# Splitting weights and values side by side: high and low parts interleaved, and another place for columns and values in each step

## The chip, the cores and the metric

The kernel runs on one core of a Trainium2 chip. The core has five engines with instruction streams of their own: TensorE (PE; its weight loads are listed apart as PEld), VectorE (DVE), ScalarE (ACT), GpSimd (POOL) and SyncE (SP), which issues transfers. They share the on-chip memory SBUF (128 partitions) and, for matmul results, PSUM. The metric is device microseconds of one execution.

## The reference, cut to what matters

An attention with random features (8 batches, 8 heads, 576 tokens, 64 values a head) is followed by a mixture of 8 experts, of which each token takes one. The change lies in the experts:

```python
x = attn_out.transpose(0, 2, 1, 3).reshape(B * S, H * D)      # 4608 x 512
logits = x @ w_gate
expert_idx = argmax(logits, axis=1)
gate_w = softmax(logits)[token, expert_idx]
for e in range(8):
    xe = x[expert_idx == e]
    h = maximum(xe @ w1[e], 0)        # 512 -> 1024
    out[expert_idx == e] = gate_w * (h @ w2[e])   # 1024 -> 512
```

All of it is fp32, and the result must be fp32 in precision.

## The kernel before, in words

The attention takes the first 270 us or so. Its tokens are written to a table in DRAM and sorted into slots by expert. The expert part then goes in steps. A step takes two blocks of 128 tokens of one expert, in a few cases three, and consists of:

- the gather of the blocks (POOL, line 855), their transposes on TensorE (line 871), and the columns: `columns` splits the transposed tokens into a high part `xh` (ScalarE, line 52) and a low part `xl` = value - high (VectorE, line 46);
- layer one, `l1`: for each of 8 slices of 128 hidden units, `products` (line 894) issues 12 matmuls into a PSUM bank: for each of 4 pieces of the 512 inputs, high weights by high columns and low weights by high columns, and then high weights by low columns. The weights are the operand that is loaded into the array, the columns (256, or 384 in a step of three blocks) are the moving operand. Lines 912 and 913 make the values: the high part `hh` by Relu on ScalarE, and the low part `hl` on VectorE, which subtracts the high part from the clipped sum;
- layer two, `l2`, for each block: 24 matmuls of 512 columns (lines 920 to 922). Here the values are what is loaded, and w2 moves: `hh` by `w2h`, `hh` by `w2l`, `hl` by `w2h`, for each of 8 pieces;
- the scaling by the gate (lines 933 and 934) and the scatter to the output (line 935).

High and low parts are of type fp32r, a form of fp32 that TensorE takes in one pass; three products of parts stand for one fp32 product. The first step's layers (lines 810 and 819) use plain fp32 instead.

The weights of an expert come by DMA into `w1s` and `w2s` (2 MB each) and are split by `split` into `w1p0`, `w1p1` (high and low of w1) and `w2p0`, `w2p1`, in 8 casts and 8 subtractions each. The order of instructions on each engine is the order of the code: in a step, `l1` of this step, then `begin` of the next (its transposes, its columns, and the split of w1 when its expert is another), then `l2` of this step. Semaphore waits are put in from the addresses that the instructions touch. The layers are written out for each step, so that addresses can differ from step to step; before, they do not. The tiles are laid one behind the other in SBUF, with two unused ones, `pad0` and `pad1`, that shift what follows.

Of the kernel before, what the change touches and what calls it, by code (L numbers as in the profile page):

```python
# [8 lines left out]
F32 = mybir.dt.float32  # L9
F32R = mybir.dt.float32r  # L10
# [8 lines left out]
P = 128  # L19
B, H, S, D, M = 8, 8, 576, 64, 128  # L20
DM = H * D
E, F = 8, 1024
# [22 lines left out]
def sub_r(nc, eng, lo, src, hi):  # L45
    eng.tensor_tensor(out=lo, in0=src, in1=hi.bitcast(F32), op=ALU.subtract)


def split_r(nc, hi, lo, src, eng_hi, eng_lo):

    if eng_hi is nc.scalar:
        nc.scalar.copy(hi, src)  # L52
    else:
        eng_hi.tensor_copy(hi, src)
    sub_r(nc, eng_lo, lo, src, hi)


class Attention:
# [318 lines left out]
    def run(self, pre):  # L377
        units = [(b, h) for b in range(B) for h in [-1] + list(range(H))]
        n, rt = len(units), self.routing
        tr = lambda i: self.unit_tr(*units[i]) if i < n else pre.rows(i - n) if i < n + 2 else None  # L380
        th = lambda i: self.unit_th(*units[i]) if i < n else None
        self.start(units)
        for b in range(B):
            i = b * (2 * NP + 1)
            if b:
                self.rest(units, i, b, pre, tr, th)
            if b + 1 < B:
                self.load_rest(b + 1)
                self.load_main(b + 1)
            for k in range(0 if b else 2, NP):  # L390
                self.pair(units, i + 1 + 2 * k, b * NP + k, pre, tr, th)
                if k == (0 if b else 2) and b + 1 < B:
                    self.load_v(b + 1)
        p = B * NP - 1
        self.pair_kv(p)
        rt.some(3)
        self.pair_fold(p - 1)
        self.unit_t(*units[n - 2])
        self.pair_fold(p, "kv")
        self.pair_nu(p - 1, 0)  # L400
        self.pair_x(p - 1, 0)
        self.unit_t(*units[n - 1])
        self.pair_nu(p - 1, 1, "tr")
        self.pair_x(p - 1, 1)
        self.pair_nu(p, 0)
        self.pair_nu(p, 1)
        self.cq.close()
        pre.banks()
        for a in range(2):
            self.pair_x(p, a)  # L410


class Routing:
# [71 lines left out]
    def bank(self, name):  # L485
        return self.ps.tile([P, 512], F32, name=name, tag=self.tag)
# [271 lines left out]
class Experts:  # L758
# [3 lines left out]
    NC, NF, T2, T3 = DM // P, F // P, 2 * P, 3 * P  # L762
# [108 lines left out]
            self.nc.tensor.transpose(p[:, c * P:(c + 1) * P], x[:, c * P:(c + 1) * P], self.ident)  # L871
        self.nc.gpsimd.tensor_copy(gate, x[:, DM:DM + 1])  # L872

    def columns(self, a, p):
        s = slice(a * P, (a + 1) * P)
        split_r(self.nc, self.xh[:, :, s], self.xl[:, :, s], p.rearrange("p (c t) -> p c t", t=P),
                self.nc.scalar, self.nc.vector)

    def xtrans(self, t):
        for a in range(2):  # L880
            self.turn(2 * t + a, self.p_x[a])
            self.columns(a, self.p_x[a])

    def third(self):
        self.turn_rows(self.x3, self.p_1[3], self.gt[6])
        self.columns(2, self.p_1[3])

    def products(self, f, o, k):

        NC, c = self.NC, slice(f * P, (f + 1) * P)  # L890
        h, l = self.xh[:, :, k], self.xl[:, :, k]
        ops = [(w, h, i) for i in range(NC) for w in (self.w1h, self.w1l)] + [(self.w1h, l, i) for i in range(NC)]
        for k, (w, x, i) in enumerate(ops):
            self.nc.tensor.matmul(o, w[:, i, c], x[:, i, :], start=k == 0, stop=k == len(ops) - 1)  # L894

    def l1(self, t, n):

        for g in range(4 if n == self.T2 else self.NF):
            if t == 1 and g < 4:
                self.split(2, range(2 * g, 2 * g + 2))  # L900
            p = self.p_1[g % 4]
            if n == self.T2:
                fs = slice(2 * g, 2 * g + 2)
                o = p.rearrange("p (f t) -> p f t", t=n)
            else:
                fs = slice(g, g + 1)
                o = p[:, :n].unsqueeze(1)
            for k, f in enumerate(range(fs.start, fs.stop)):
                for c in (slice(0, self.T2), slice(self.T2, n)) if n > self.T2 and g == 0 else (slice(0, n),):
                    self.products(f, o[:, k, c], c)  # L910
            a, b = self.hh[:, fs, :n], self.hl[:, fs, :n]
            self.nc.scalar.activation(a, o, AF.Relu)  # L912
            self.nc.vector.scalar_tensor_tensor(out=b, in0=o, scalar=0.0, in1=a.bitcast(F32), op0=ALU.max,  # L913
                                                op1=ALU.subtract)

    def l2(self, t, a):
        nc, k = self.nc, slice(a * P, (a + 1) * P)
        h, l, p = self.hh, self.hl, self.p_2[a % 2]
        for c in range(self.NF):
            nc.tensor.matmul(p, h[:, c, k], self.w2h[:, c, :], start=c == 0, stop=False)  # L920
            nc.tensor.matmul(p, h[:, c, k], self.w2l[:, c, :], start=False, stop=False)  # L921
            nc.tensor.matmul(p, l[:, c, k], self.w2h[:, c, :], start=False, stop=c == self.NF - 1)  # L922
        if a == 2:
            self.send(p, self.y3, self.gt[6], self.idx[:, 2 * NPR + t:2 * NPR + t + 1])
        else:
            self.store(2 * t + a, p, self.idx)
# [31 lines left out]
    def step(self, t, following):  # L958
        engines = (ET.PE, ET.DVE, ET.Activation, ET.Pool)
        two = self.reg(5, t, 1, engines)  # L960
        with self.tc.If(two > 0) as pair:  # L961
            self.l1(t, self.T2)
        with pair.Else():
            self.third()
            self.l1(t, self.T3)
        if t + 2 < NPR:
            self.gather(t + 2)
        if t + 1 < NPR:
            self.gather3(t + 1)
        if t == 1:  # L970
            self.next(0, 2)
        following()
        self.nc.gpsimd.drain()  # L973
        with self.tc.If(two > 0) as pair:  # L974
            self.l2(t, 0)
            self.when(self.reg(4, t, 1, engines), lambda: self.l2(t, 1))
        with pair.Else():
            for a in range(3):
                self.l2(t, a)
# [11 lines left out]
    def run(self, ctx):  # L991
        nc, rt = self.nc, self.rt
        cp = ctx.enter_context(self.tc.tile_pool(name="mo_c", bufs=1))
        NC, NF, T2 = self.NC, self.NF, self.T2
        bank = lambda n, tags: [self.ps.tile([P, 512], F32, name=f"{n}{i}", tag=g) for i, g in enumerate(tags)]
        self.p_2 = bank("p_2", ("tr", "nu"))
        self.p_x = bank("p_x", ("kv", "t2"))
        ring = lambda n, sh, dt, k: [cp.tile(sh, dt, name=f"{n}{i}") for i in range(k)]
        cp.tile([P, 88], F32, name="pad0")
        (self.w1h, self.w1l), (self.w2h, self.w2l) = (ring(n, [P, c, w], F32R, 2) for n, c, w in  # L1000
                                                      (("w1p", NC, F), ("w2p", NF, DM)))
        self.h0 = cp.tile([P, NF, T2], F32, name="h0")
        self.hh, self.hl = (cp.tile([P, NF, self.T3], F32R, name=n) for n in ("hh", "hl"))
        cp.tile([P, 48], F32, name="pad1")
        self.xh, self.xl = (cp.tile([P, NC, self.T3], F32R, name=n) for n in ("xh", "xl"))
        self.ys = ring("ys", [P, DM], F32, 3)
        xg = ring("xgm", [P, ROW], F32, 2)
        self.x3, self.y3 = cp.tile([P, ROW], F32, name="x3"), cp.tile([P, DM], F32, name="y3")
        for x in xg + [self.x3]:
            nc.gpsimd.memset(x, 0.0)  # L1010
        self.xg = self.xg + xg

        rt.slots(cp, (self.p_2[0], self.p_x[0], self.p_x[1]), self.idx, lambda: self.fill(22))
        self.fill(32)
        self.gather(1)
        self.gather3(1)
        self.gather(2)
        for g in range(4):
            self.relu0(g)
        rt.plan(self.flags)  # L1020
        self.split(1)
        self.next(0, 1)
        self.l20(0)
        self.xtrans(1)
        self.l20(1)
        for t in range(1, NPM - 1):
            if t > 1:
                self.change(t, 2)
            self.step(t, lambda: self.begin(t + 1))
        self.tail(NPM - 1)  # L1030
# [45 lines left out]
```

## Time and profile before

| | us |
|---|---|
| three runs: lowest, median, highest | 729.4, 730.23, 730.68 |
| the profiled execution | 732.33 |
| its span, first to last instruction | 730.6 |
| TensorE busy | 706.3 (97%) |
| VectorE busy | 380.4 (52%) |
| ScalarE busy | 325.5 (45%) |
| GpSimd busy | 256.4 (35%) |

The duration of a matmul in the profile is the time from its start to its modelled end, and matmuls overlap; what a matmul takes of the time is the distance from its start to the start of the next. In a row of the timeline that merges several instructions, the second number is the time from the start of the first to the end of the last.

### The profile page before, as it was taken

Reading aid. Unit: us, or ns where it says so; the run is one execution under the profiler, and the core shown is the slowest. Engines: PE = TensorE matmul, PEld = TensorE weight load, DVE = VectorE, ACT = ScalarE, POOL = GpSimd, SP = SyncE. Lnnn points to the kernel's source line nnn. Section 1 sums busy time; section 2 is a strip of 40 time slices with the busy share of each in tenths; the row PEclk is TensorE's granted clock in tenths of the full one; section 3 lists DMA queues with packets and bytes.
Section 4 is the critical chain, followed back from the end, with each engine's and each line's share of the span. In section 5 each row is a group of like instructions: output and inputs, shape, how many; then the busy total and the mean of one; then the engine's idle time right before and its main releaser. Section 6 shows DMA issues by size and latency. Waiting matters only on the chain. (4 is left out here: it accounts for less than half of the span.)

```text
span 730.6 us, 18640 instructions
## 1 busy us (share of the span) xinstructions
PE 706.3 (97%) x6985; PEld 632.5 (87%) x6985; DVE 380.4 (52%) x860; ACT 325.5 (45%) x950; POOL 256.4 (35%) x459
## 2 busy tenths in 40 slices
PE   7999999999999999999999999999998999999995
PEld 6898889888888887788999889998987989989994
DVE  4689899899899888722221245212343245122220
ACT  6877887877778735411221144212342144111210
POOL 7555555555546633221222112221112303211221
PEclk9999999999999999999999999999999999999998
DMA  8944735626633611551111026121144125201000
GB/s 209 261 121 114 215 109 157 196 69 197 196 115 121 227 62 40 182 174 37 46 52 59 32 83 230 61 70 37 31 144 168 61 85 194 80 31 34 17 32 22
DMA packets 69502, 79.82 MB, mean 109 GB/s; under 512 B 28398, under 2 KB 52974, under 8 KB 69360
## 3 DMA queue, kind: packets, MB, share of 16 engines
q1 hardware_dynamic: 61136, 58.81, 26.1%
q0 software_dynamic: 7680, 19.04, 7.9%
q8 instruction: 82, 1.34, 0.8%
q14 instruction: 60, 0.49, 0.2%
q10 hardware_dynamic: 544, 0.13, 0.1%
HBM read 64.79 MB, written 19.55 MB: 115 GB/s over the span
## 5 line engine op out<-in xcount | busy, mean ns | idle before, releaser
L894 PE MATMUL p<-xh,w1p 128*128 128x256 f32 (+2 forms) x1104 | 159.5, 287 | 0.9 <-ACT xh L52 0.9
L894 PEld LDWEIGHTS p<-xh,w1p 128*128 128x128 f32 x1104 | 146.0, 189 | 2.9 <-ACT xh L52 1.3
L935 POOL DMA_INDIRECT out_dram<-ys,idx x36 | 36.9, 1026 | 305.4 <-DVE ys L934 213.3
L913 DVE SCALAR_TENSOR_TENSOR hl<-p,hh 128x512 fp32r<-128x512 f32 (+1 forms) x76 | 50.1, 662 | 135.2 <-ACT hh L912 133.0
L920 PE MATMUL p<-w2p,hh 128*128 128x512 f32 x288 | 114.3, 397 | 3.1 <-DVEq L940 2.7
L921 PE MATMUL p<-w2p,hh 128*128 128x512 f32 x288 | 112.9, 392 | 0.0
L922 PE MATMUL p<-w2p,hl 128*128 128x512 f32 x288 | 112.8, 392 | 0.0
L912 ACT ACTIVATE hh<-p 128x512 fp32r<-128x512 f32 (+1 forms) x76 | 43.8, 576 | 142.6 <-PE p L894 140.1
L934 DVE TENSOR_SCALAR ys<-p,gt 128x256 f32<-128x256 f32 x36 | 17.4, 482 | 153.1 <-ACT ys L933 153.1
L186 ACT ACTIVATE kp<-pp,mx 128x128 f32<-128x128 f32 x256 | 76.2, 417 | 44.5 <-DVE mx L176 29.2
L933 ACT ACTIVATE ys<-p,gt 128x256 f32<-128x256 f32 x36 | 17.1, 476 | 170.9 <-PE p L922 103.2
L894 PE MATMUL p<-xl,w1p 128*128 128x256 f32 (+2 forms) x552 | 90.7, 287 | 0.0
L176 DVE TENSOR_REDUCE mx<-pp 128x8 f32<-128x1024 f32 x64 | 76.9, 1214 | 7.7 <-PE pp L169 4.5
L186 ACT ACTIVATE qp<-pp,mx 128x128 f32<-128x128 f32 x256 | 78.4, 457 | 0.0
L203 POOL TENSOR_TENSOR k<-kp 128x256 f32<-128x256 f32 x64 | 46.7, 730 | 88.2 <-ACT kp L186 81.7
L894 PEld LDWEIGHTS p<-xl,w1p 128*128 128x128 f32 x552 | 77.4, 190 | 0.1
L169 PE MATMUL pp<-om_t,th 64*128 64x128 f32 x1024 | 70.8, 283 | 1.3 <-ACT th L156 0.7
L169 PEld LDWEIGHTS pp<-om_t,th 64*128 64x128 f32 x1024 | 61.6, 187 | 9.8 <-issue 5.5
L920 PEld LDWEIGHTS p<-w2p,hh 128*128 128x128 f32 x288 | 54.4, 189 | 14.3 <-issue 3.5
L922 PEld LDWEIGHTS p<-w2p,hl 128*128 128x128 f32 x288 | 54.5, 189 | 11.6
L921 PEld LDWEIGHTS p<-w2p,hh 128*128 128x128 f32 x288 | 54.5, 189 | 10.9
L264 PE MATMUL nu<-kva,qt 128*64 128x73 f32 x1024 | 42.9, 229 | 3.7 <-ACT kva L251 3.5
(370 smaller groups left out, 1086.9 us busy)
## 6 DMA issues: line engine op xcount, KB each, us to landing
w1s<-in_moe_w_dram SPq DMA_DIRECT2D x5, 2048.0 KB, 8.7
w2s<-in_moe_w_dram SPq DMA_DIRECT2D x5, 2048.0 KB, 10.3
v<-in_v_dram SPq DMA_DIRECT2D x32, 256.0 KB, 5.5
token_rows<-xc SPq DMA_DIRECT2D x8, 1024.0 KB, 5.1
k<-in_k_dram SPq DMA_DIRECT2D x31, 256.0 KB, 5.1
q<-in_q_dram SPq DMA_DIRECT2D x31, 256.0 KB, 5.5
kr<-in_k_dram SPq DMA_DIRECT2D x16, 64.0 KB, 2.6
vz<-in_v_dram SPq DMA_DIRECT2D x16, 64.0 KB, 5.6
```

Source lines behind the costliest of these rows:

```text
L169: nc.tensor.matmul(pp[:, a, n, i, :], th[r, c], self.om[r, :], start=True, stop=True)
L176: nc.vector.tensor_reduce(out=mx[:, :, n], in_=s[("pp", h)][:, :, n], axis=AX.X, op=ALU.max, negate=True)
L186: nc.scalar.activation(x[:, j, :], pp[:, j % 2, n, j // 2, :], AF.Exp, bias=mx[:, j % 2, n, j // 2:j // 2 + 1])
L203: add = lambda o, x, y: nc.gpsimd.tensor_tensor(out=o, in0=x, in1=y, op=ALU.add)
L264: nc.tensor.matmul(o[r, j, :], qt[:, j, r], kva[:, a, :], start=True, stop=True)
L894: self.nc.tensor.matmul(o, w[:, i, c], x[:, i, :], start=k == 0, stop=k == len(ops) - 1)
L912: self.nc.scalar.activation(a, o, AF.Relu)
L913: self.nc.vector.scalar_tensor_tensor(out=b, in0=o, scalar=0.0, in1=a.bitcast(F32), op0=ALU.max, op1=ALU.subtract)
L920: nc.tensor.matmul(p, h[:, c, k], self.w2h[:, c, :], start=c == 0, stop=False)
L921: nc.tensor.matmul(p, h[:, c, k], self.w2l[:, c, :], start=False, stop=False)
L922: nc.tensor.matmul(p, l[:, c, k], self.w2h[:, c, :], start=False, stop=c == self.NF - 1)
L935: self.nc.gpsimd.indirect_dma_start(out=self.out[:, :], in_=y, in_offset=None, bounds_check=NT - 1, out_offset=bass.IndirectOffsetOnAxis(a ...
```

## The change: high and low side by side, and a place that moves

w1's two parts become one tile, in which the low part of each element stands right behind its high part. The values' two parts are joined in the same way. Both are read and written through views with a step of two elements; the values between them are the other part. w2's parts and the columns' parts stay tiles of their own. The columns `xh`, `xl` and the values `hp` get 128 elements more, and in step t they begin at an offset within these: a multiple of 8 elements (32 bytes) given by (t - 1) * 3 mod 16 for the columns and (t - 1) * 5 mod 16 for the values. The order of the tiles in SBUF changes (columns ahead of the values).

```diff
+    def col(self, t):
+        o = (t - 1) * 3 % 16 * 8
+        return [x[:, o:o + self.NC * self.T3].rearrange("p (c n) -> p c n", n=self.T3) for x in (self.xh, self.xl)]
+
+    def mid(self, t):
+        o = (t - 1) * 5 % 16 * 8
+        x = self.hp[:, o:o + self.NF * self.T3 * 2].rearrange("p (f n s) -> p f n s", n=self.T3, s=2)
+        return x[:, :, :, 0], x[:, :, :, 1]
+
-    def columns(self, a, p):
+    def columns(self, t, a, p):
         s = slice(a * P, (a + 1) * P)
-        split_r(self.nc, self.xh[:, :, s], self.xl[:, :, s], p.rearrange("p (c t) -> p c t", t=P),
+        split_r(self.nc, *(x[:, :, s] for x in self.col(t)), p.rearrange("p (c t) -> p c t", t=P),
                 self.nc.scalar, self.nc.vector)
...
-    def products(self, f, o, k):
+    def products(self, t, f, o, k):
 
         NC, c = self.NC, slice(f * P, (f + 1) * P)
-        h, l = self.xh[:, :, k], self.xl[:, :, k]
+        h, l = (x[:, :, k] for x in self.col(t))
...
-            a, b = self.hh[:, fs, :n], self.hl[:, fs, :n]
+            a, b = (x[:, fs, :n] for x in self.mid(t))
             self.nc.scalar.activation(a, o, AF.Relu)
...
     def l2(self, t, a):
         nc, k = self.nc, slice(a * P, (a + 1) * P)
-        h, l, p = self.hh, self.hl, self.p_2[a % 2]
+        (h, l), p = self.mid(t), self.p_2[a % 2]
...
         cp.tile([P, 88], F32, name="pad0")
-        (self.w1h, self.w1l), (self.w2h, self.w2l) = (ring(n, [P, c, w], F32R, 2) for n, c, w in
-                                                      (("w1p", NC, F), ("w2p", NF, DM)))
+        w1p = cp.tile([P, NC, F, 2], F32R, name="w1p")
+        self.w1h, self.w1l = w1p[:, :, :, 0], w1p[:, :, :, 1]
+        self.w2h, self.w2l = ring("w2p", [P, NF, DM], F32R, 2)
+        cp.tile([P, 48], F32, name="pad1")
+        self.xh, self.xl = (cp.tile([P, NC * self.T3 + P], F32R, name=n) for n in ("xh", "xl"))
         self.h0 = cp.tile([P, NF, T2], F32, name="h0")
-        self.hh, self.hl = (cp.tile([P, NF, self.T3], F32R, name=n) for n in ("hh", "hl"))
-        cp.tile([P, 48], F32, name="pad1")
-        self.xh, self.xl = (cp.tile([P, NC, self.T3], F32R, name=n) for n in ("xh", "xl"))
+        self.hp = cp.tile([P, NF * self.T3 * 2 + P], F32R, name="hp")
```

The instructions of each engine stay the same and in the same order. Only waits on ScalarE and VectorE differ, since they follow from addresses. On ScalarE, where a step begins the next one (the two casts of columns, then the casts of w1), the program before has:

```order
L52 CAST xh<-p_x_5515 128x4x128 [waits DVE_49,PE_49]
L52 CAST xh<-p_x_5516 128x4x128 [waits DVE_49,PE_49]
L843 TENSOR_LOAD flags
L940 COMPARE_AND_BRANCH
L52 CAST w1p_5518<-w1s 128x512 [waits DMAHW3_49,DMAHW5_49,DMAHW1_49,DMAHW7_49,DVE_49,Activation_49]
L52 CAST w1p_5518<-w1s 128x512 [waits DVE_49,Activation_49] x7
```

The same place now, in one of the steps:

```order
L52 CAST xh<-p_x_5515 128x4x128 [waits DVE_49,PE_49,Activation_49]
L52 CAST xh<-p_x_5516 128x4x128 [waits PE_49]
L843 TENSOR_LOAD flags
L949 COMPARE_AND_BRANCH
L52 CAST w1p<-w1s 128x512 [waits DMAHW5_49,DMAHW7_49,DMAHW3_49,DMAHW1_49]
L52 CAST w1p<-w1s 128x512 x7
```

A cast of columns now waits for ScalarE's own earlier work (in most steps the second of the two, here the first), and the casts of w1 no longer name VectorE and ScalarE.

## Rows read from the trace of the kernel before

**Rows 1.** The page: busy time by engine, and TensorE's granted clock in 40 slices.
```profile
PE 706.3 (97%) x6985; PEld 632.5 (87%) x6985; DVE 380.4 (52%) x860; ACT 325.5 (45%) x950; POOL 256.4 (35%) x459
PEclk9999999999999999999999999999999999999998
```

**Rows 2.** Busy time by stretch: stretch, length, engines, granted clock, DMA share, GB/s.
```profile
300.00:350.00 50.00, 50.00 (x339) 46.20 (x338) 15.27 (x26) 13.73 (x26) 12.69 (x16) 1.00 0.38 131
...
461.11:472.43 11.32, 11.32 (x97) 11.28 (x96) 2.56 (x4) 2.27 (x4) 4.36 (x6) 1.00 0.23 72
438.10:449.45 11.35, 11.35 (x98) 11.31 (x96) 7.28 (x12) 6.43 (x12) 4.81 (x6) 1.00 0.61 219
```

**Rows 3.** Groups, shapes kept apart: count, busy us, mean ns, idle before.
```profile
L894 PE MATMUL p<-xh,w1p 128*128 128x256 f32 x976 | 135.4, 282 | 0.0
...
L920 PE MATMUL p<-w2p,hh 128*128 128x512 f32 x288 | 114.3, 397 | 3.1 <-DVEq L940 2.7 <-PEq L940 0.4
...
L894 PE MATMUL p<-xl,w1p 128*128 128x256 f32 x488 | 77.4, 281 | 0.0
...
L894 PE MATMUL p<-xh,w1p 128*128 128x384 f32 x112 | 21.9, 337 | 0.0
...
L894 PE MATMUL p<-xl,w1p 128*128 128x384 f32 x56 | 12.0, 336 | 0.0
```

**Rows 4.** Timeline, layer one of 256 columns: start us, us, engine, group.
```profile
462.75 1.10 PE L894 MATMUL p<-xh,w1p 128*128 128x256 f32 x8
...
466.52 0.64 PE L894 MATMUL p<-xl,w1p 128*128 128x256 f32 x4
...
469.82 1.10 PE L894 MATMUL p<-xh,w1p 128*128 128x256 f32 x8
```

**Rows 5.** Timeline, layer two: the third matmul of two triples.
```profile
452.95 0.39 PE L922 MATMUL p<-w2p,hl 128*128 128x512 f32 x1
...
461.11 0.39 PE L922 MATMUL p<-w2p,hl 128*128 128x512 f32 x1
```

**Rows 6.** Timeline, steps of three blocks: first groups, then groups of 384 columns.
```profile
508.92 0.62 PE L894 MATMUL p<-xl,w1p 128*128 128x256 f32 x4
...
572.34 0.62 PE L894 MATMUL p<-xl,w1p 128*128 128x256 f32 x4
...
577.09 1.55 PE L894 MATMUL p<-xh,w1p 128*128 128x384 f32 x8
...
587.49 1.55 PE L894 MATMUL p<-xh,w1p 128*128 128x384 f32 x8
```

**Rows 7.** Timeline, weight loads: plain fp32 of 512 columns, one each; transposes.
```profile
293.60 0.19 PEld L819 LDWEIGHTS p<-w2s,h 128*128 128x128 f32 x1 [0.24 <-issue]
...
298.75 0.19 PEld L819 LDWEIGHTS p<-w2s,h 128*128 128x128 f32 x1 [0.24 <-issue]
...
472.55 0.89 PEld L871 LDWEIGHTS p_x<-ident,xgm 128*128 128x128 f32 x8
```

**Rows 8.** VectorE reductions, by line: duration min/median/max; L490's elements lie 288 bytes apart.
```profile
L490 DVE TENSOR_REDUCE rt_L<-x x8: 620/623/628, 52.3 to 269.1; 128x32 f32<-128x256 f32 x8
L696 DVE TENSOR_REDUCE f_tt<-rt_L x1: 453/453/453, 276.1 to 276.1; 128x36 f32<-128x288 f32 x1
```

**Rows 9.** Timeline, what covers ScalarE and VectorE around the two layers.
```profile
292.11 4.89 DVE L46 TENSOR_TENSOR w1p<-w1s,w1p 128x512 fp32r<-128x512 f32 x8
...
297.32 1.27 DVE L46 TENSOR_TENSOR xl<-p_x,xh 128x512 fp32r<-128x512 f32 x2
...
299.21 1.51 PE L894 MATMUL p<-xh,w1p 128*128 128x256 f32 x8
...
450.43 0.69 DVE L913 SCALAR_TENSOR_TENSOR hl<-p,hh 128x512 fp32r<-128x512 f32 x1 [2.14 <-ACT hh L912]
...
592.03 4.89 DVE L46 TENSOR_TENSOR w1p<-w1s,w1p 128x512 fp32r<-128x512 f32 x8
...
606.79 0.99 PE L894 MATMUL p<-xh,w1p 128*128 128x256 f32 x7
```

More of the change, by code (lines that the diff above doesn't have):

```diff
@@ L881, in xtrans, with third @@
             self.turn(2 * t + a, self.p_x[a])
-            self.columns(a, self.p_x[a])
-    def third(self):
+            self.columns(t, a, self.p_x[a])
+    def third(self, t):
         self.turn_rows(self.x3, self.p_1[3], self.gt[6])
-        self.columns(2, self.p_1[3])
-    def products(self, f, o, k):
+        self.columns(t, 2, self.p_1[3])
+    def products(self, t, f, o, k):
         NC, c = self.NC, slice(f * P, (f + 1) * P)
-        h, l = self.xh[:, :, k], self.xl[:, :, k]
+        h, l = (x[:, :, k] for x in self.col(t))
         ops = [(w, h, i) for i in range(NC) for w in (self.w1h, self.w1l)] + [(self.w1h, l, i) for i in range(NC)]
@@ L909, in l1 @@
                 for c in (slice(0, self.T2), slice(self.T2, n)) if n > self.T2 and g == 0 else (slice(0, n),):
-                    self.products(f, o[:, k, c], c)
-            a, b = self.hh[:, fs, :n], self.hl[:, fs, :n]
+                    self.products(t, f, o[:, k, c], c)
+            a, b = (x[:, fs, :n] for x in self.mid(t))
             self.nc.scalar.activation(a, o, AF.Relu)
@@ L963, in step @@
         with pair.Else():
-            self.third()
+            self.third(t)
             self.l1(t, self.T3)
```

## The prediction

> **What bounds the kernel now.** I read the page's busy shares first, then the busy time by stretches, then the groups with shapes kept apart, and last single stretches of the timeline, because only those give the distance from one matmul to the next. TensorE is busy for 97% of the span and its clock is at the higher level (2.4 GHz) in nearly every slice [rows 1]. In the expert part, from about 299 us to the end, it is busy 50.00 of 50 us, while VectorE has 15.27 and ScalarE 13.73 [rows 2]. So the only thing that can move the end by much is how closely the matmuls of the two expert layers follow each other. The reader is to take three distances from the rows:
>
> - First layer, 256 columns: a group of 12 matmuls starts at 462.75 and the sixth group at 469.82, so 7.07 us / 60 = 117.8 ns [rows 4]. There are 976 + 488 = 1464 of them [rows 3].
> - First layer, 384 columns (the steps of three blocks): (587.49 - 577.09) / 60 = 173.3 ns [rows 6]; 112 + 56 = 168 matmuls [rows 3].
> - Second layer, 512 columns: twelve triples from 452.95 to 461.11, so 8.16 us / 36 = 226.7 ns [rows 5]; three lines of 288, so 864 matmuls [rows 3].
>
> From 384 to 512 columns the distance grows by 53.4 ns for 128 columns, 0.417 ns a column, which is one column a cycle of 2.4 GHz. Then 512 columns need 213.3 ns, and 13.4 ns a matmul are something else. The plain fp32 matmuls of line 819 (512 columns as well, with a weight load of the same size before each) follow each other every (298.75 - 293.60) / 12 = 429.2 ns [rows 7], and twice 213.3 is 426.7: only 2.5 ns over. So the 13.4 ns are no fixed price of changing weights; they come up where the moving operand is read at a column a cycle while the next weights are being read. A weight load alone needs (0.89 - 0.14) / 7 = 107 ns for 128 elements, by the transposes [rows 7]. At 256 columns load and matmul are about equally long (107 and 106.7), both disturb each other, and the distance is 117.8.
>
> Two more rows tell what this disturbance is like. It does not depend on the other engines: the step at 438.10 has 7.28 us of VectorE, 6.43 of ScalarE and DMA at 0.61, the one at 461.11 has 2.56, 2.27 and 0.23, and both take 11.3 us for their 96 matmuls [rows 2]. And it is not one number: at the start of the two three-block steps, with the same addresses, four matmuls take 0.62 us where a usual group takes 0.64 [rows 4, 6]; less the 0.28 us of the last one, that is 113 ns a matmul against some 120 (rounding leaves 3 ns either way). So the distance depends on how the two reads happen to stand to each other in time.
>
> **The change, part by part.** No instruction is added, removed or moved on any engine; PE, POOL and SP keep their waits too. What changes is where three tiles lie, and the step between elements.
>
> (a) The weight operand of both expert layers (w1 in the first, the values in the second) is read with a step of two elements. Per matmul the weight read then passes over 1024 bytes in place of 512. At 107 ns that is 9.6 bytes per ns, just what the moving read does (2048 bytes in 213.3 ns). No row shows a weight read with such a step, so its price needs bounds. From below: two reads of equal pace that collide once are out of each other's way from then on, where reads at a ratio of 1 to 2 meet again and again. If the excess goes to the 2.5 ns of line 819, the second layer wins 10.9 x 864 = 9.4 us and the 384-column matmuls 10.9 x 168 = 1.8 us. At 256 columns the nearest row is the 113 ns, which wins 117.8 - 113.3 = 4.5 x 1464 = 6.6 us; the lowest end is the transposes' 107, 10.8 x 1464 = 15.8 us. Sum: -17.8 us, at most -27. From above: VectorE's reduction of line 490 reads single elements 288 bytes apart in 623 ns for 256, and line 696 reads 288 adjoining ones in 453 [rows 8]: 2.43 against 1.57 ns an element, a factor of 1.55. With it a weight load takes 166 ns. That lies below the second layer's 226.7, but the first layer waits for it: 59 x 1464 = +86 us, and nearly nothing at 384 columns. I take the gain, since the rows of TensorE lie nearer than a VectorE row with 36 times the step.
>
> The Trainium skill ("SBUF — State Buffer", the section on Door 1, the note on cachelines) says that SBUF is read in lines of 16 bytes and that two hits a line suffice for full speed. A step of two fp32 leaves just two, so by it the +86 us do not arise; no run here shows it. A second rule speaks against my gain: by "TensorE: Matmul & The Clock Gate", Part 2, weights have a read port of their own and loading them takes no read bandwidth from the running matmul. By it there is nothing to win and the time stays at 730; the 13.4 ns beside the 2.5 ns disagree with it as far as they go.
>
> (b) ScalarE and VectorE write w1 and the values, and VectorE reads the high part back, with the step of two. With the factor of 1.55 a w1 subtraction goes from 0.60 us (4.89 / 8) to 0.95, eight of them 2.7 us longer. In the loop that ends at 599.6 in place of 596.9, and the next first layer starts at 606.79 [rows 9]: hidden under the second layer. At the first step the eight start at 292.11, the low columns follow until 298.59, and the first matmul starts at 299.21 [rows 9]; the low columns are wanted after eight matmuls (1.51 us less the last one's tail), so about 0.8 us would show. The low part of the last pair of values ends at 450.43 + 0.69 = 451.1 [rows 9], and its first matmul is the 19th of 48, at 461.11 - 29 x 0.2267 = 454.5: 0.6 us more is covered by the 18 before it. I take 0 for (b), with +0.8 as the other end.
>
> (c) Columns and values start at another multiple of 32 bytes in each step. Nothing is computed for it at run time. Tiles of neighbouring steps now overlap at shifted places, so one cast of columns waits for the cast before it on its own engine, which could cost the overlap of the two, some 0.1 us a step, behind which the subtraction and then the w1 casts stand; all of it lies beside the second layer's 11 us. Its other effect is on how the two reads stand to each other. The two levels at equal addresses, 113 and 118, bound it: between -6.6 us, which (a) already has, and nothing.
>
> (d) The waits that w1 and w2 casts lose were on work long done; 0.
>
> Sum: 732.3 (the profiled execution) - 17.8 = 714.5. The median of the three runs is 2.1 us below the profiled one, so I say **712.5 us**. Within this case 703 (the transposes' level) to 723 (only half of it comes).
>
> **The rivals.**
>
> Nothing changes. If the 13.4 ns come from the type of the operands alone, an element read costs the same wherever it lies, and (b) is hidden: 730.2 us. For it: the distance of 117.8 is the same in steps with quite different traffic [rows 2]. Against it: 113 ns at the same operands [rows 6]. The first rule against the gain leads here.
>
> Slower: each piece of memory that the weight read opens costs the moving read something, and with the step of two it opens twice as many. Place: every expert matmul. Price: the excess doubles, 13.4 x (864 + 168) = 13.8 us, and in the first layer 117.8 - 107 = 10.8 x 1464 = 15.8 us; 732.3 + 29.6 - 2.1 = 760 us. It decides from the point where the reads do not fall into step; if it holds for a part of the steps only, the time lies between 732 and 760. For it: the excess exists only where both reads run. Against it: other engines' reads cost TensorE nothing, so that not simply any further access does.
>
> Slower by much: the read with the step takes 1.55 times as long (+86 us, 816 us), or twice (a first-layer distance of 118 + 107 = 225 ns, 1464 x 107 = +157 us and 168 x 52 = +9 us, 894 us). Against it: the moving read already passes over as many bytes in the time.
>
> The change does what it says in the layout, but in some steps the new place is worse and in others better: 725 to 735 us, part of the first two cases.
>
> **How the numbers follow.** The gain 0.50; nothing 0.17; the excess doubled, fully or in part, 0.25; the slow read 0.08. About 0.2% (1.5 us) is what a measurement of this kernel tells from no change. So faster 0.50, same 0.17, slower 0.33. The range of 704 to 758 leaves out the slow read, the full doubling and the very end of the gain. Since cases of both signs hold much of the chance, the likeliest one's own range of 703 to 723 stands beside it.
>
> **What would show it.** In the profile of the changed kernel: the second layer's distance at 216 in place of 226.7, the 384-column one at 163, the first layer's at 113 or below, alike in all steps. Distances that differ from step to step would show that the place decides, against the pace. Distances of 240 and 128 would be the doubled excess, 177 or 225 at 256 columns the slow read. If ScalarE's and VectorE's groups of w1 and of the values are longer, (b) is priced, and a wait of TensorE for VectorE at 300 us would be its cost. I am wrong if the distances stay as they are.

## The result and the profile after

The changed kernel takes 738.55 us (median of 4 runs, 736.86 to 741.21), the kernel before 730.45 us beside it: 1.011 times as long, interval 1.0074 to 1.015. It is slower, where 712.5 us and faster were forecast. The profiled execution took 739.51 us with a span of 737.7, against 732.33 and 730.6.

First the page of the changed kernel, the lines that answer to [rows 1]: busy time by engine, and TensorE's clock in 40 slices.

```profile
PE 713.6 (97%) x6985; PEld 642.3 (87%) x6985; DVE 379.9 (52%) x860; ACT 328.7 (45%) x950; POOL 256.6 (35%) x459
PEclk9999999999999999999999999999999999999998
```

The same 6985 matmuls take 7.3 us more, their weight loads 9.8 us more; VectorE and POOL stand where they stood. A stretch by windows (columns as in [rows 2]) shows TensorE as full as before, with 328 matmuls in the 50 us where there were 339:

```profile
300.00:350.00 50.00, 50.00 (x328) 46.31 (x328) 15.24 (x25) 13.37 (x25) 12.03 (x15) 1.00 0.37 125
```

So the time went where the prediction looked for it, into the distance from one matmul to the next. The groups with shapes kept apart answer to [rows 3] (count, busy us, mean ns, idle before). The mean durations grow by 1 to 3 ns, and the one wait for VectorE's queue stays (2.5 us, 2.7 before):

```profile
L903 PE MATMUL p<-xh,w1p 128*128 128x256 f32 x976 | 137.8, 283 | 0.0
L929 PE MATMUL p<-w2p,hp 128*128 128x512 f32 x288 | 115.3, 400 | 2.9 <-DVEq L949 2.5 <-PEq L949 0.4
```

The distances themselves come from the timeline. Below are pairs of group starts (start us, us, engine, group), as in [rows 4 to 6]. A stretch is the unbroken run of a layer's matmuls in one step, and its level is the distance that it settles on. First, layer one in two steps: five groups of 12 from 464.87 to 472.06 are 7.19 us / 60 = 119.8 ns a matmul, and six groups from 348.31 to 357.03 are 121.1; [rows 4] gave 117.8.

```profile
348.31 1.13 PE L903 MATMUL p<-xh,w1p 128*128 128x256 f32 x8
...
357.03 1.13 PE L903 MATMUL p<-xh,w1p 128*128 128x256 f32 x8
...
464.87 1.13 PE L903 MATMUL p<-xh,w1p 128*128 128x256 f32 x8
...
472.06 1.13 PE L903 MATMUL p<-xh,w1p 128*128 128x256 f32 x8
```

Layer two, the third matmul of triples, in two steps: fifteen triples from 359.83 to 370.43 are 235.6 ns a matmul, from 407.16 to 417.51 they are 230.0; [rows 5] gave 226.7 in every step.

```profile
359.83 0.40 PE L931 MATMUL p<-w2p,hp 128*128 128x512 f32 x1
...
370.43 0.40 PE L931 MATMUL p<-w2p,hp 128*128 128x512 f32 x1
...
407.16 0.39 PE L931 MATMUL p<-w2p,hp 128*128 128x512 f32 x1
...
417.51 0.40 PE L931 MATMUL p<-w2p,hp 128*128 128x512 f32 x1
```

The 384-column groups go from 173.3 ns [rows 6] to (528.61 - 518.01) / 60 = 176.7:

```profile
518.01 1.57 PE L903 MATMUL p<-xh,w1p 128*128 128x384 f32 x8
...
528.61 1.58 PE L903 MATMUL p<-xh,w1p 128*128 128x384 f32 x8
```

All stretches of a layer added up (each from its first matmul to the start of what follows it), layer one takes 211.0 us in place of 207.1, and layer two 202.4 in place of 199.2; all else together is 324.3 in both. That is the 7.1 us of the spans. Layer two lost more than 3.2 us: in the kernel before, the 2.7 us wait was followed by a stretch at a lower clock, by this row of its windows, where 13 matmuls took 4.41 us in place of 13 x 0.2267 = 2.95.

```profile
558.38:562.79 4.41, 4.41 (x13) 3.47 (x13) 0.00 (x0) 0.00 (x0) 0.00 (x0) 0.61 0.08 27
```

The changed kernel has the wait but not the lower clock behind it (1.00 from 548 to 575 us). Without these 1.5 us, layer two lost 4.6 us (3.16 + 1.46).

### The profile page after: what moved, and what is told of

Its sections match the earlier page's. It is cut to its first block, busy times and chain, and to the rows that moved or that the text cites. A ratio compares the mean times of both kernels' runs of the same rounds, so it can differ in the third digit from the quotient of the medians.

```text
span 737.7 us, 18569 instructions
## 1 busy us (share of the span) xinstructions
PE 713.6 (97%) x6985; PEld 642.3 (87%) x6985; DVE 379.9 (52%) x860; ACT 328.7 (45%) x950; POOL 256.6 (35%) x459
## 5 line engine op out<-in xcount | busy, mean ns | idle before, releaser
L903 PE MATMUL p<-xh,w1p 128*128 128x256 f32 (+2 forms) x1104 | 162.3, 289 | 0.3 <-ACT xh L52 0.3
L903 PEld LDWEIGHTS p<-xh,w1p 128*128 128x128 f32 x1104 | 149.8, 196 | 2.3 <-ACT xh L52 0.7
L922 DVE SCALAR_TENSOR_TENSOR hp<-p,hp 128x512 fp32r<-128x512 f32 (+1 forms) x76 | 50.1, 663 | 140.7 <-ACT hp L921 127.8
L929 PE MATMUL p<-w2p,hp 128*128 128x512 f32 x288 | 115.3, 400 | 2.9 <-DVEq L949 2.5
L930 PE MATMUL p<-w2p,hp 128*128 128x512 f32 x288 | 113.7, 395 | 0.0
L931 PE MATMUL p<-w2p,hp 128*128 128x512 f32 x288 | 113.6, 395 | 0.0
L921 ACT ACTIVATE hp<-p 128x512 fp32r<-128x512 f32 (+1 forms) x76 | 46.8, 615 | 145.2 <-PE p L903 139.2
L903 PEld LDWEIGHTS p<-xl,w1p 128*128 128x128 f32 x552 | 79.2, 196 | 0.1
L929 PEld LDWEIGHTS p<-w2p,hp 128*128 128x128 f32 x288 | 56.3, 196 | 13.4 <-issue 3.2
L931 PEld LDWEIGHTS p<-w2p,hp 128*128 128x128 f32 x288 | 56.2, 195 | 10.8
L930 PEld LDWEIGHTS p<-w2p,hp 128*128 128x128 f32 x288 | 56.4, 196 | 10.1
```

## The experiments

The expectations name four theories. A: reading weights with a step of two costs something in itself. B: the places cost, not the step. C: the moving operand's read and the read of the next weights meet in SBUF; step, place and what ran just before set how often, and how they stand to each other at a stretch's start is kept through it. D: operands alone decide; what ran before, or where columns begin, does not matter.

**One part at a time.** In e1 only w1 is interleaved, in e2 only the values between the layers, in e4 both, all at fixed places as in the kernel before; e3 has the moving places and interleaves nothing.

```
e1:  w1p = tile([P, NC, F, 2]);        w1h, w1l = w1p[:, :, :, 0], w1p[:, :, :, 1]
e2:  hp  = tile([P, NF, T3, 2]);       hh, hl   = hp[:, :, :, 0], hp[:, :, :, 1]
e4:  both lines
e3:  o = (t - 1) * 3 % 16 * 8;  xh[:, o:o + NC * T3] ...    o = (t - 1) * 5 % 16 * 8;  hh[:, o:o + NF * T3] ...
```

> Only w1's high and low parts are interleaved; columns and values lie where they lay before, at the same place in every step. Theory A (the step of two costs in itself, because the weight read opens twice as much memory, and the place adds only a few ns): the first layer's distance goes from 117.8 to about 120 ns, the second layer stays at 226.7; 1464 x 2.3 ns = +3.4 us, about 734 us. Theory B (the place costs, the step is free): both distances stay, 730 us.

> Only the values are interleaved; w1's parts are apart and every place is the one of before. Theory A: the second layer's distance goes from 226.7 to about 233 ns, the first layer stays at 117.8; 864 x 6.5 ns = +5.6 us, about 736 us. Theory B: both stay, 730 us.

> Nothing is interleaved; columns and values (two tiles of values) take the changed kernel's places, another one in each step. Theory A: distances move by a ns or two at most, 729 to 732 us. Theory B: the whole slowdown is here, 738 us, and the distances differ from step to step as in the changed kernel.

> Both interleaved, as in the changed kernel, but columns and values at the one place that they have before. Theory C (two reads of TensorE meet in SBUF; the step and the place set how often, and how the two reads stand to each other when a stretch begins is kept through it): the layers do what they did apart, 120.0 ns in the first and about 234.5 in the second; 1464 x 2.2 + 864 x 5.8 = +8.3 us, about 737 us, so that the moving place adds nothing on the whole. Theory B' (the moving place carries the part that neither interleaving explains): clearly faster than the changed kernel, 730 us or less.

| kernel | us, median | before beside it | ratio, interval | layer one, 256 columns | layer two |
|---|---|---|---|---|---|
| e1, w1 | 733.85 | 729.19 | 1.0056 [1.0037, 1.0075] | 120.0 in every step | 226.7 |
| e2, values | 726.28 | 729.19 | 0.9967 [0.9947, 0.9988] | 113.4 in every step | 233.3 |
| e3, places | 734.10 | 729.19 | 1.005 [1.0029, 1.0071] | 113.3 to 120.0 by step | 226.7 to 234.2 by step |
| e4, both steps | 739.99 | 728.93 | 1.013 [1.0089, 1.0172] | 120.0 in every step | 233.3 |

e1 came as A said. In e2 layer two came as A said too (233.3), but the kernel got faster, which no theory had; e3 lies between A (729 to 732) and B (738); e4 came out 3 us above what C gave.

These medians hold more than the two layers. A stretch of 3.4 us at a granted clock of 0.5, in the layer two behind the wait, stands in the profiles of e1, e3, e4 and the kernel before, and not in that of e2. The mean granted clock of an execution is 0.994 or 0.995 in the profiles with it and 0.997 or 0.998 in the others; by that mark it was in 6 of 10 executions of e1, 1 of 10 of e2, 7 of 10 of e3 and 3 of 4 of e4, but in only 7 of the 25 and 2 of the 7 of the kernel before beside them. The two layers by themselves, added up as above and without the 1.5 us, differ from the kernel before by +3.4 us (e1), -1.1 (e2), +3.6 (e3) and +8.9 (e4). So interleaving alone, at fixed places, brings the whole of what the changed kernel lost in its layers (3.9 + 4.6 = 8.5 us).

The timelines behind the table, one fence a kernel. e1, six groups of layer one (8.65 / 72 = 120.1 ns) and nine triples of layer two (6.13 / 27 = 227.0):

```profile
462.39 1.12 PE L894 MATMUL p<-xh,w1p 128*128 128x256 f32 x8
...
471.04 1.12 PE L894 MATMUL p<-xh,w1p 128*128 128x256 f32 x8
...
473.58 0.40 PE L921 MATMUL p<-w2p,hh 128*128 128x512 f32 x1
...
479.71 0.39 PE L921 MATMUL p<-w2p,hh 128*128 128x512 f32 x1
```

e2, twelve triples (8.40 / 36 = 233.3), then six groups of layer one (8.16 / 72 = 113.3):

```profile
450.30 0.39 PE L921 MATMUL p<-w2p,hp 128*128 128x512 f32 x1
...
458.70 0.39 PE L921 MATMUL p<-w2p,hp 128*128 128x512 f32 x1
...
460.54 1.07 PE L894 MATMUL p<-xh,w1p 128*128 128x256 f32 x8
...
468.70 1.07 PE L894 MATMUL p<-xh,w1p 128*128 128x256 f32 x8
```

e3, layer one in two neighbouring steps: (472.94 - 464.30) / 72 = 120.0, then (495.98 - 487.82) / 72 = 113.3:

```profile
464.30 1.12 PE L902 MATMUL p<-xh,w1p 128*128 128x256 f32 x8
...
472.94 1.12 PE L902 MATMUL p<-xh,w1p 128*128 128x256 f32 x8
...
487.82 1.07 PE L902 MATMUL p<-xh,w1p 128*128 128x256 f32 x8
...
495.98 1.07 PE L902 MATMUL p<-xh,w1p 128*128 128x256 f32 x8
```

e1, e2 and e4 show that the step costs 2.2 ns in layer one and 6.6 in layer two at the places of the kernel before, and e3 shows that the places without the step cost as much in many steps; neither A nor B holds alone. The parts do not add up (in the medians +4.7 us, -2.9, and +11.1 for both at once; in the layers +3.4, -1.1 and +8.9). The reason is the surprise in e2: layer one runs at 113.3 ns though its operands, their addresses and all its instructions are those of the kernel before, where it ran at 117.8. Only what ran ahead of it, layer two with the step, is different. That speaks for C and against D, and it was not expected.

**The reads by themselves.** Four micro kernels run only stretches of such matmuls, in their own tiles, each in one execution, while no other engine computes. The first varies the step, the second the place, the other two what stands ahead of a stretch.

```
m1:  matmul(bank[:, :n], wt[:, step * 128 * (i % 4) ...: step], mv[:, 0:n])       x49 each, step 1, 2, 3, 4, 8; also mv with step 2
m2:  matmul(bank[:, :n], wt[:, 128 * (i % 4) ...],       mv[:, o:o + n])          x37 each, o = 0, 2, 4, 8, 12, 16, 24 ... 120
```

> Only stretches of 25 to 49 matmuls with a weight load each; nothing of the reference is computed. fp32r, moving 512, 384, 256 and 64 columns, weights read with a step of 1, 2, 3, 4 and 8 elements; two stretches with a moving step of two, two of plain fp32. Theory A: at 512 columns the distance is about 227 at step 1, 233 at step 2, more at step 4 (a new piece of memory for each element) and the same at 8; at 64 columns, where the load alone sets the distance, steps 1 and 2 are equal (about 110). Theory B: steps 1 and 2 are equal at every width.

> Only stretches of 37 matmuls, nothing of the reference: fp32r, 512 or 256 columns, weights with a step of 1 or 2, and the moving operand beginning at 0 to 120 elements in 19 places. Theory C: the distance at 512 columns goes with the place, between 215 and 236 ns at step 1, in a pattern that repeats; at 256 columns it takes a few levels from 113 to 121. Theory D (the place has nothing to do with it): 226.7 and 120 everywhere at step 1, 233.3 and 120 at step 2.

m1's timeline, one row a stretch of 49; the distance is the start of the next stretch less its own, by 49. 512 columns at step 1 (L31) and 2 (L32): 226.7 and 233.5. 256 columns at step 1, 2 and 4 (L39 to L41): 119.6, 120.0 and 233.5; at step 3 (L48) 172.4. Columns read with a step of two: 234.3 in L50, whose first half has a granted clock of 0.5, and 230.0 in L51, where the clock is 1.00 throughout and the weights have a step of two as well. The 25 plain fp32 matmuls of a stretch leave 50 records; by the length of their groups less the last record's 0.59 us, these follow each other every 429.6 ns at step one (L52) and 429.2 at step two (L53).

```profile
21.84 11.27 PE L31 MATMUL bank<-mv,wt 128*128 128x512 f32 x49
32.95 11.60 PE L32 MATMUL bank<-mv,wt 128*128 128x512 f32 x49
44.39 11.68 PE L33 MATMUL bank<-mv,wt 128*128 128x512 f32 x49
...
108.22 6.03 PE L39 MATMUL bank<-mv,wt 128*128 128x256 f32 x49
114.08 6.04 PE L40 MATMUL bank<-mv,wt 128*128 128x256 f32 x49
119.96 11.60 PE L41 MATMUL bank<-mv,wt 128*128 128x256 f32 x49
131.40 11.99 PE L42 MATMUL bank<-mv,wt 128*128 128x256 f32 x49
...
197.24 8.61 PE L48 MATMUL bank<-mv,wt 128*128 128x256 f32 x49
205.69 10.09 PE L49 MATMUL bank<-mv,wt 128*128 128x64 f32 x49
215.59 11.66 PE L50 MATMUL bank<-mv,wt 128*128 128x256 f32 x49
227.07 11.46 PE L51 MATMUL bank<-mv,wt 128*128 128x256 f32 x49
238.34 21.64 PE L52 MATMUL bank<-src 128*128 128x512 f32 x50
259.82 21.62 PE L53 MATMUL bank<-src 128*128 128x512 f32 x50
```

A weight read with a step of two keeps its pace: at 256 columns, where load and matmul are equally long, it costs 0.4 ns at most. At 64 columns, where the load alone sets the distance, the granted clock fell to 0.5 within the stretch of step one (from 111.7 to 213.3 ns), and step two, all of it at 0.5, gave 213.3 as well. With a step of four the load is half as fast. So the upper bound of the prediction (166 ns a load) is refuted for a step of two. At 512 columns, steps of four and eight gave 235.0 and 244.6, where A had them equal.

m2's timeline, stretches of 37 with the weights at step 1. 512 columns beginning at element 0 (L31), 2 (L32) and 64 (L42): 226.8, 233.5 and 227.0; 256 columns at element 0 (L50) and 48 (L59): 119.5 and 113.8, the levels at the stretch's end being 120.0 and 113.3.

```profile
21.88 8.55 PE L31 MATMUL bank<-mv,wt 128*128 128x512 f32 x37
30.27 8.81 PE L32 MATMUL bank<-mv,wt 128*128 128x512 f32 x37
38.91 8.73 PE L33 MATMUL bank<-mv,wt 128*128 128x512 f32 x37
...
116.36 8.55 PE L42 MATMUL bank<-mv,wt 128*128 128x512 f32 x37
124.76 8.80 PE L43 MATMUL bank<-mv,wt 128*128 128x512 f32 x37
...
185.06 4.59 PE L50 MATMUL bank<-mv,wt 128*128 128x256 f32 x37
189.48 4.60 PE L51 MATMUL bank<-mv,wt 128*128 128x256 f32 x37
...
224.46 4.37 PE L59 MATMUL bank<-mv,wt 128*128 128x256 f32 x37
228.67 4.54 PE L60 MATMUL bank<-mv,wt 128*128 128x256 f32 x37
```

At step 1 most places of the 512 columns give 231.5 to 234.2 ns; only 0 and 64 give 226.7, and 16 and 80 give 229. The pattern repeats after 64 elements (256 bytes); at 256 columns it does so with one exception, element 8 (116.7) against 72 (117.8). At step 2 eleven of the 19 places give 233.3 (230.0 to 235.4 in all), and at 256 columns all lie between 118.3 and 121.3: none reaches the 113.3 that e2 found in layer one, and e4, with w1 interleaved too, did not have it. The PSUM bank of the result does not decide: the same bank took 226.8 from element 0 and 234.3 from element 40. So the kernel before stood at a good place in layer two, and the change took it away twice: by the step, and by moving it (there the change moves the weights, while m2 moves the columns). The levels of the kernels come without any other engine at work, so the slower casts of ScalarE are not needed for them.

**What runs ahead of a stretch.** m3 lets stretches of 24 matmuls of 512 columns and 36 of 256 take turns as the layers do, with different things between; m4 does so with other places of the 256 columns.

> Only blocks of 24 matmuls of 512 columns followed by 36 of 256 columns, nothing of the reference; operands of the 256-column part at the same place in most blocks, and what stands between the two parts varies (nothing, one matmul of 32 to 384 columns, one of plain fp32, weights with a step of two in the part before). Theory C: the 256-column distance is 113.3, 117.8 or 120 by what stands before, at equal operands. Theory D: the same distance in all of them, and what differs between the kernels lies elsewhere.

> Micro kernel: stretches of 24 products of 512 columns and 36 of 256 by turns, as the layers; what stands in front of the 256-column stretch or where its columns begin differs. Columns at elements 48 and 48 again: 117.8 ns, as measured twice before. Theory C: columns at other elements (4 to 60) give one of a few levels between 113.3 and 120 by the place alone, and at least one may be 113.3 directly; first product cut in two (64+192, 96+160, 128+128): 113.3 for those that end the entry at the same offset as a product of 64 or 96 between, 117.8 for others; one of 80 between: 113.3, one of 112: either. Theory D: 117.8 in all that begin at 48.

m3's rows (the direct entry at element 48 stands four times in m3 and twice in m4, at 117.8 each time): layer one entered directly (L32), behind one matmul of 96 columns (L43), behind one of 128 (L46), and behind layer two with the step (L71).

```profile
26.79 4.40 PE L32 MATMUL bank<-mv,wt 128*128 128x256 f32 x36
31.03 5.60 PE L33 MATMUL bank<-mv,wt 128*128 128x512 f32 x24
...
65.68 4.32 PE L43 MATMUL bank<-mv,wt 128*128 128x256 f32 x36
...
75.35 4.45 PE L46 MATMUL bank<-mv,wt 128*128 128x256 f32 x36
...
163.39 4.25 PE L71 MATMUL bank<-mv,wt 128*128 128x256 f32 x36
```

Entered directly, 36 matmuls take 31.03 - 26.79 = 4.24 us, 117.8 ns each, as in the kernel before. The groups' own lengths, all with the same tail of the last matmul, are 4.40, 4.32, 4.45 and 4.25 us; the single records level out at 117.8, 113.3, 117.8 and 113.3, the last as in e2 (the two in the middle begin with one longer distance, behind the short matmul). One matmul of 64, 80, 96, 192, 320 or 384 columns between gives 113.3 as well, one of 32, 112, 128, 160, 224 or 256 leaves 117.8. m4 adds that the columns' place decides with it: directly entered, element 28 gives 113.3, elements 8 and 36 give 116.7, all others tried 117.2 to 120.0. A product cut in two ahead of the stretch gave 113.3 for 128 + 128 and 117.8 for 64 + 192 and 96 + 160; I had expected it the other way round. C says that the entry counts, then, but it did not foretell which entry gives which level.

**Back in the kernel.** If C holds, the kernel before can be made faster with nothing interleaved. e5 and e6 put one matmul between, of 96 columns (which should help) and of 128 (which should not); e7 only moves layer one's columns to element 28; e8 is e7 with one matmul more in the three-block steps.

```
e5:  +  if g == 0 and n == self.T2:
     +      matmul(p[:, :96], w1h[:, 0, :P], xh[:, 0, :96], start=True, stop=True)
e6:  the same with 128 for 96
e7:  -  xh, xl = (tile([P, NC, T3]) ...)
     +  xh, xl = (tile([P, NC * T3 + 64])[:, 28:28 + NC * T3] ...)
e8:  e7, and the matmul of e6 where n == self.T3
```

> The kernel before with nothing interleaved, and one product more ahead of each layer one of a two-block step (256 columns): 96 columns, whose result the next product overwrites. Theory C (the moving read and the read of the next weights meet in SBUF, and how they stand to each other at the start of a stretch is kept through it): a product of 96 columns between the layers moved the micro kernel from 117.8 to 113.3 ns, and cost 34 ns less over 36 products than going over directly, so 299 ns less over 96: 14 stretches are entered directly from layer two, 14 x 0.299 = 4.2 us less than before, about 725.0 beside 729.2; layer one at 113.3-113.4 ns, layer two unchanged at 226.7. Theory D (the operands alone decide a product's time): layer one stays at 117.8 and the product added costs 0.04-0.10 us, 15 times: 0.7-1.6 us more, 730-731.

> As e5_one_between, but the added product has 128 columns. Theory C as the micro kernel measured it: behind one of 128 columns layer one ran at 117.75 ns as directly, and the stretch was 112 ns longer, so 14 x 0.112 = 1.6 us more than before, about 730.8, layer one at 117.8. Theory D: the same within its bounds (730-731), so the two theories part only by the difference of e5_one_between and this kernel: 5.8 us by C, under 0.5 us by D. If any extra product helped (for instance because it gives the first real product time), both would be faster.

> The kernel before with nothing interleaved and nothing added; only the place of layer one's columns is another, for the whole kernel: they begin 28 elements behind a multiple of 64 elements instead of 48. Theory C, from the micro kernel: entered directly from layer two, columns at 28 run at 113.33 ns from the second third of a stretch on, and 36 of them took 4.118 us instead of 4.240; over 96 that is 0.121 + 60 x 0.00442 = 0.386 us less a stretch, 14 stretches: 5.4 us, so 724.1 beside 729.5, with the one wait of 2.7 us in front of a layer two at 555-558 us and the lower clock behind it (1.5 us) still there; 720 if that wait goes as it did in e5_one_between and e6_one_of_128. The 384-column products' place is new and not priced: 192 products, up to 1 us either way. Theory D (places matter by alignment to a line of 16 bytes at most, 28 and 48 being both multiples of four elements): no difference, 729.5.

> As e7_columns_28, with one product of 128 columns more ahead of layer one in the two three-block steps only, which shifts the instructions behind it by as many places in each step's code as the added product of e5_one_between and e6_one_of_128 did. If the wait at 555-558 us hangs on where the code lies, it is gone here (720, 4.2 us below e7_columns_28 if that has it); if it hangs on the added product standing in front of the two-block step itself (its time), it stays, and the kernel takes as long as e7_columns_28 plus 2 x 0.1 us.

| kernel | us, median | before beside it | ratio, interval | layer one, at a stretch's end |
|---|---|---|---|---|
| e5, one of 96 | 722.50 | 729.49 | 0.9911 [0.9894, 0.9928] | 113.3 |
| e6, one of 128 | 728.52 | 729.49 | 0.9982 [0.9973, 0.9992] | 117.8 |
| e7, element 28 | 722.72 | 729.51 | 0.9907 [0.9882, 0.9932] | 113.3 |
| e8, 28 and one | 721.18 | 729.51 | 0.9882 [0.9859, 0.9905] | 113.3 |

Timelines of e5 (8.16 / 72 = 113.3) and e6 (8.48 / 72 = 117.8), six groups of layer one:

```profile
459.82 1.07 PE L894 MATMUL p<-xh,w1p 128*128 128x256 f32 x8
...
467.98 1.07 PE L894 MATMUL p<-xh,w1p 128*128 128x256 f32 x8
```

```profile
461.96 1.10 PE L894 MATMUL p<-xh,w1p 128*128 128x256 f32 x8
...
470.44 1.10 PE L894 MATMUL p<-xh,w1p 128*128 128x256 f32 x8
```

e5 and e6 differ by 6.0 us (5.8 expected by C, under 0.5 by D), with the same instructions but for 32 columns of one matmul in each two-block step. D has fallen. That the two reads meet in SBUF itself, as C words it, no run shows apart from these distances. Both came out some 2.5 us below what was expected, which fits the wait of 2.7 us ahead of one layer two [rows 3] being gone in both (the lower clock behind it was in only 3 of the 16 executions of the kernel before, so its median hardly holds that). e7 has a shorter one at the same place, by its waits (us in total, times, longest us), and e8 has none:

```profile
PE p L920 <- ACTq L940: 1.1, 1, 1.1
```

Layers one and two take 201.2 and 197.8 us in both e7 and e8 (e8's added matmuls included), and all else 321.9 and 320.6; so e8's gain over e7 is that wait for the most part. In both kernels with the added matmul of the two-block steps it is gone, and in e8, whose matmul stands in code that the step in question does not run. That fits a dependence on where code lies, but the three differ in time too, and nothing that holds the code's place alone was run; its cause stays open. e8 is the fastest kernel here: 0.988 times the kernel before, where the changed kernel takes 1.011 times as long. Of its gain of 8.3 us, layer one's level is 5.9 us (207.1 to 201.2), and the wait most of the rest; in e5 layer one, the added matmuls included, gained 4.6 us of 7.0.

## Why the prediction was wrong, by its steps

**What bounds the kernel** was right: all of the difference lies in the matmul distances of the two layers, TensorE is as full as before, and the 13.4 ns and 10.8 ns over a column a cycle hang on both reads: m1 moves the distance by the weights' step alone, m2 by the columns' place alone. That this interplay has levels that depend on how the reads stand to each other was seen in the 113 ns groups, and the runs bear it out.

**(a) is the step that failed**, in its lower bound, which I took as the value: that two reads of equal pace which collide once are out of each other's way from then on, so that the excess goes to 2.5 ns. The excess at 512 columns did not fall from 13.4 ns but rose to 20 (233.3 less 213.3, e2, e4 and m1), and at 256 columns from 117.8 to 120.0 (e1, e4). In place of -17.8 us stand layer one's +3.9 us and layer two's +4.6 us. The argument rested on the plain fp32 row, whose 429.2 ns are the distance of records that move 512 columns at half the pace, as slowly as their weights are read. m1 has the same records with weights at step two, at twice the moving read's pace, and they keep 429.2 ns: equal pace was not what freed that row of excess. One reading of the rise, not shown by itself, is that a weight read with a step of two opens twice the memory in the same time, and meets the moving read more often or at a worse moment; the micro kernels show the sum (226.7 to 233.3), not the single collision. The rival that came out is the "excess doubled in part": its full price of 30 us was too high by three to four times, because in layer one the excess rose by only 2.2 ns of 11, and in layer two by half.

The upper bound of 86 us fell, as I had held likely: 0.4 ns, not 59, at 256 columns in m1. The rule of the Trainium skill ("SBUF — State Buffer", Door 1, cachelines: two hits a line suffice) agrees for the weight read, 120.0 ns at step two against 233.5 at step four. It does not hold for the moving columns, which took 230.0 at step two (L51 of m1) against 119.6. The other rule of the Trainium skill, that loading weights takes no read bandwidth from the running matmul ("TensorE: Matmul & The Clock Gate", Part 2), disagrees with m1: the same columns took 226.7 or 233.5 by the step of the weights alone.

**(b)** was right: the cover held. ScalarE's casts of w1 went from 616 to 671 ns and its values from 598 to 641, VectorE's stayed (680 to 684, 690 to 691), so VectorE's factor of 1.55 at 288 bytes did not carry over to 8. The first matmul of the expert part starts at 299.16 us, and no later (299.21 before).

**(c)** was mis-sized in sign. I bounded the places by -6.6 us and nothing, from the two levels that the trace showed at one place. It shows nothing of worse places, and e3's two layers take 3.6 us more for them alone (734.10 us in all, inside the 725 to 735 of the rival on places): layer two at 226.7 to 234.2 ns where it had 226.7. The 0.1 us a step for the two casts of columns did not come: in the median they start 0.46 us apart, 0.47 before. What I overlooked is that equal distances in every step [rows 5] are also what a single, good place looks like.

**(d)** was right: TensorE's waits in the expert part stayed as they were, 2.5 us in place of 2.7 being the longest.

**The chances.** Slower had 0.33, of which 0.25 lay on the case that came; 738.55 us lies inside the range, which says little for the working, since the range took in cases of both signs. Two of its numbers do not follow from its sums: half of the gain gives 732.3 - 8.9 - 2.1 = 721 us, not 723, and the load twice as long gives 896 us, not 894. Neither changes a chance. The mark "distances that differ from step to step would show that the place decides" came true in part (230 to 236 ns in layer two of the changed kernel, where e4, at fixed places, has 233.3 in every step).

## What to carry to other kernels

When TensorE is full, measure the distance of equal matmuls in every stretch, and take a level that never varies as one draw of several, not as a floor. Before changing a layout for the two reads of TensorE, try the cheap draws: another start of the moving columns within 256 bytes, or one small matmul ahead of a stretch; here they made the kernel 0.9 to 1.2% faster, 0.6 to 0.8% by layer one's level and the rest by a wait that shortened or went, whose cause is open, while the layout lost 1.1%. Which draw is good was found by trying, not foretold. And an argument that two periodic accesses fall into step needs a row that shows it.

## What the runs showed of the hardware

- At equal operands and instructions, a stretch of 256-column matmuls runs at 113.3 or 117.8 ns by what ran just ahead of it (m3, e2, e5, e6), and keeps the level that it settles on to its end, 96 matmuls in the kernel.
- The columns' start counts, in a pattern that repeats after 256 bytes at seven of eight places at 256 columns (113.3 to 120 ns) and at all eight at 512 (226.7 to 234 ns, within 1 ns; m2).
- These matmuls read weights at full pace with a step of two but not of three (172.4) or four (233.5 ns at 256 columns); the moving columns take 230.0 ns, about half their pace, at a step of two already (m1, L51).
- Plain fp32 matmuls of 512 columns leave two records each, 429 ns apart, at a weight step of one and of two alike (m1).
- In the profile of the kernel before, a wait of TensorE of 2.7 us was followed by 4.4 us at a mean granted clock of 0.61, and so were waits of 2.3, 2.1 and 2.2 us in those of e1, e3 and e4 (a granted clock of 0.5 for 3.4 us); one of 2.5 us in the changed kernel and one of 1.9 in e2 were not. So the length of the wait alone does not decide it.
- Not tried: whether only the difference of the two operands' places counts. m2 and e7 move the columns, whereas in layer two the change moves the weights.
